# A recurrence and attention kernel: two triangular inverses, a table of side jobs and one copy rearranged

## The chip, the cores and the metric

The kernel runs on one core of a Trainium2 chip. A core has five engines that run their own instruction streams side by side and wait for each other by semaphores: TensorE (PE, matmuls and transposes), VectorE (DVE), ScalarE (ACT), GpSimd (POOL) and SyncE (SP, which issues the transfers here). The metric is the time of one execution on the device in microseconds (us). The profile comes from one execution.

## The reference

There are two parts. The first is a linear recurrence over 768 time steps, for 4 batches of 8 heads, each with a 40 x 40 state; the second is causal attention by four experts of which two are chosen per token.

```
for t in range(S):
    y[:, :, t] = np.einsum('bhd,bhde->bhe', rt, state)
    Sa = np.einsum('bhde,bhe->bhd', state, at)
    state_decay = state * wt[:, :, None, :] - np.einsum('bhd,bhe->bhde', Sa, bt)
    state = state_decay + np.einsum('bhd,bhe->bhde', vt, kt)
...
logits = x @ w_gate                       # x: y as (4, 768, 320)
topk = np.argpartition(-logits, K, axis=-1)[..., :K]
...
for e in range(E):
    q = x @ wq[e]; k = x @ wk[e]; v = x @ wv[e]
    ... causal softmax(q k^T / 8) ...
    ye = a @ v @ wo[e]
    # added to the tokens that chose e, with their weight
```

## The kernel before, in words

**Tiling.** Time is cut in 24 chunks of 32 steps; four chunks are a window, so there are 6 windows W. The 32 heads (batch x head) are 4 groups g of 8. A *unit* u = 4c + g is one chunk of one group: 96 units. Within a chunk the recurrence is written with 32 x 32 matrices: a unit needs the inverse of a triangular one for each head, and the state that the unit of the chunk before has left.

**Units.** A loop over n does one phase each of several units (MAIN): in this order u of unit n-1 (matmul with the inverse TT, L370), g of unit n (L362), y of unit n-3 (the product with the states, L390), f of unit n-2 (matmul L382, then masked on DVE, L383), the transposes t (L414), k (L351) and v of unit n-1 (L377). ACT copies between them from PSUM: GT (L364), R (L372), VU (L378), the state (L400), LS (L355, L418). The decay (L402, DVE) turns py into the output XT.

**Preps.** What a group's units of a window need is prepared beforehand, in 24 preps i = 4W + g, each a string of small pieces that have letters: `a` a scan of 528 columns (L257), `b` a copy of four of its columns, PC (L259), `c` their reciprocal (L261), `s` a second scan SC (L263), `x`/`y` two products AB (L266; `X`/`Y` the same on POOL), `p` the keys KB on POOL (L268) or `k`/`l` the same in two halves on DVE (L271), `d`/`q` copies into GL on ACT (L273), `m`/`n` eight matmuls AB by KB each (L279) with a mask on DVE into GL (L280), `o` a store of a part of GL to DRAM, Ld (L284). `w`, `v`, `e` load EW, EA and EK for the next prep: EK has one buffer.

**The inverse of a window** (`invert`): its 128 triangular matrices lie one to a partition. `L` loads Ld into MT and LT (L297, L298), then for j = 1 to 30 a row step adds a multiple of row j to the rows before it: a product (L309) and a sum (L311). The rows are split at kp = 11: the first 11 on POOL (`tp`), the others on DVE (`td`); for window 0 it is the other way round, and DVE's 11 rows are split again in two chains that are written alternately (KS = 5). `S` stores the result to DRAM (Td, L313), `R` (or `B` in window 0) loads it back, transposed, in four transfers (TT, L316).

**What sets the order.** Every engine executes its instructions in the order in which the code emits them. START is a list of the pieces ahead of the first unit (`4no` means pieces n and o of prep 4, `T28` 28 rounds of row steps). EARLY, SIDE, SIDE1 (W = 1) and SIDE2 (W = 2) are tables of pieces that are put into the loop: in SIDE tables row r stands for iteration 16(W-1) + r (row steps, `S` and `R` 16 later), and the slashes part the seven phases of an iteration; `t2` is two row steps on DVE. Phase 3 is f. POOL's row steps of window W are spread evenly over the first iterations of the window before.

**The attention part** follows from about 440 us on. A check on the inputs' spread, the *verdict* (a few small DVE instructions and a PE transpose, L871), stands at its start.

Of the kernel before, what the change touches and what calls it, by code (L numbers as in the profile page):

```python
# [137 lines left out]
def recurrence(tc, ctx, I, xT, CM, early, tail=None, KP=(11, 11, 11, 11, 11, 11)):  # L138
# [30 lines left out]
    GL = [t[:, 0:4096].rearrange("p (g n s t) -> p g n s t", g=4, n=16, s=2) for t in GF]  # L169
# [77 lines left out]
    def prep(i):  # L247

        w, g = divmod(i, NG)
        AB, sc, kb, pc = ABr[i % 4], SC[i % 12], KB[i % NKB], PC[i % 12]  # L250
        gl = GL[w % 2]
        SUF = SUFs[1 if i in (1, 3, 5) else 0]
        sv = SUF[:, 1:529].rearrange("p (n c) -> p n c", c=33)
        EW, EA, EK = (x[0:104] for x in (E8[i] if i < 8 else own))
        ea = EA.rearrange("p (n c) -> p n c", c=32)
        def f0a():
            V.tensor_tensor_scan(SUF[:, 0:528][:, ::-1], EW[:, ::-1], d1[:, ::-1], 1.0, op0=OP.mult, op1=OP.add)  # L257
        def f0b():
            V.tensor_copy(pc, sv[:, ::4, 0])  # L259
        def f0c():  # L260
            V.reciprocal(D1P[:, 0:528:132], pc)  # L261
        def f1():
            V.tensor_tensor_scan(sc.rearrange("p n c -> p (n c)"), EW, D1P, 0.0, op0=OP.mult, op1=OP.add)  # L263
        def f2(s, e=V):
            q = slice(64 * s, 64 * s + 40)
            e.tensor_tensor(AB[q, :, 32 * s:32 * s + 32], ea[q], sc[q, :, 0:32], op=OP.mult)  # L266
        def fp():
            PL.tensor_tensor(kb[0:104].rearrange("p n (k c) -> p n k c", k=2), EK.rearrange("p (n k c) -> p n k c", n=16, k=2),  # L268
                             sv[:, :, None, 1:33].to_broadcast([104, 16, 2, 32]), op=OP.mult)
        def fk(k):  # L270
            V.tensor_tensor(kb[0:104, :, 32 * k:32 * k + 32], EK.rearrange("p (n k c) -> p n k c", n=16, k=2)[:, :, k], sv[:, :, 1:33], op=OP.mult)  # L271
        def f5(s):
            A.activation(gl[64:104, g, :, s, :], AB[64 * s:64 * s + 40, :, 32 * s:32 * s + 32], AF.Copy)  # L273
        def mm(c):
            p_a = ps([64, 4, 2, 64])
            for p in range(4):
                for cc in range(2):
                    n = p * 4 + c + cc
                    T.matmul(p_a[:, p, cc, :], kb[0:104, n, :], AB[0:104, n, :], start=True, stop=True)  # L279
            V.tensor_tensor(gl[0:64, g].rearrange("q (p c) s t -> q p c s t", p=4)[:, :, c:c + 2].rearrange("q p c s t -> q p (c s) t"),  # L280
                            p_a.rearrange("q p c (s t) -> q p (c s) t", s=2), maskn[:, None, None, :].to_broadcast([64, 4, 4, 32]),
                            op=OP.mult)
        def f6():
            nc.sync.dma_start(Ld[w % 2][32 * g:32 * g + 32].rearrange("n j t -> j n t"),  # L284
                              gl[32:64, g].rearrange("q n s t -> q (n s) t"))
        def load(k):
            load_e(i + 1, k)
        return dict(a=f0a, b=f0b, c=f0c, s=f1, x=lambda: f2(0), X=lambda: f2(0, PL), y=lambda: f2(1), Y=lambda: f2(1, PL), p=fp, k=lambda: fk(0), l=lambda: fk(1),
                    d=lambda: f5(0), q=lambda: f5(1), m=lambda: mm(0), n=lambda: mm(2), o=f6,
                    w=lambda: load(0), v=lambda: load(1), e=lambda: load(2))  # L290

    def invert(w):

        L, M = LT, MT
        kp = KP[w]
        def ld():
            nc.sync.dma_start(M, Ld[w % 2])  # L297
            nc.sync.dma_start(L, Ld[w % 2][:, kp:31])  # L298
        def cp():
            PL.memset(M.rearrange("p t j -> p (t j)")[:, ::33], 1.0)  # L300
        def step(e, j, r0, r1, tmp):

            m, n = min(j, r1) - r0, 31 - j
            if m <= 0:
                return []
            tmp = tmp[:, 0:n * m].rearrange("p (t i) -> p t i", t=m)
            o = M[:, r0:r0 + m, j + 1:32]
            row = L[:, j - kp, j + 1:32] if j >= kp and r1 <= kp else M[:, j, j + 1:32]
            return [lambda: e.tensor_tensor(tmp, row[:, None, :].to_broadcast([128, m, n]),  # L309
                                            M[:, r0:r0 + m, j][:, :, None].to_broadcast([128, m, n]), op=OP.mult),  # L310
                    lambda: e.tensor_tensor(o, o, tmp, op=OP.add)]  # L311
        def st():
            nc.sync.dma_start(Td[w % 2], M)  # L313
        def bk():
            for g in range(4):
                nc.sync.dma_start(TT[w % 2][32 * g:32 * g + 32], Td[w % 2][32 * g:32 * g + 32].rearrange("n t j -> t n j"))  # L316
# [23 lines left out]
    def unit(u):  # L340
# [15 lines left out]
        def s_g():  # L356
            p_g = ps([97, 4, 40])
            for h in range(8):
                p, s = divmod(h, 2)
                o = 1024 * g + 64 * (p * 4 + cw) + 32 * s  # L360
                r = 104 * (h0 // 2 + p) + 64 * s
                T.matmul(p_g[64 * s:64 * s + 33, p], gl[:, o:o + 33], r1[:, r:r + 40], start=True, stop=True, tile_position=(0, 64 * s))  # L362
            for s in range(2):
                A.activation(gt[32 * g:32 * g + 32, s::2], p_g[64 * s:64 * s + 32], AF.Copy)  # L364
        def s_u():
            p_u = ps([97, 4, 40])
            for h in range(8):
                p, s = divmod(h, 2)
                o = 64 * (p * 4 + cw) + 32 * s
                T.matmul(p_u[64 * s:64 * s + 33, p], tt[:, o:o + 33], gt[:, h, :], start=True, stop=True, tile_position=(0, 64 * s))  # L370
            for s in range(2):
                A.activation(hd(r2[32:64, 40 * h0:40 * h0 + 320], 40)[:, s::2], p_u[64 * s:64 * s + 32], AF.Copy, scale=-1.0)  # L372
# [129 lines left out]
    for n in range(NU + 4):  # L502
# [4 lines left out]
        for s, (x, d) in enumerate(MAIN):  # L507
# [140 lines left out]
def moe(tc, ctx, I, xT, out, ident, pre, FL=None, FI=None):  # L648
# [241 lines left out]
    for n in range(N + LAG[2]):  # L890
# [78 lines left out]
```

## Time and profile before

| | us |
|---|---|
| median of 3 runs | 694.3 (690.43 to 698.01) |
| the profiled execution's own time | 693.77 |
| its span on the core | 691.9 |
| PE busy | 578.5 (84%) |
| DVE busy | 513.7 (74%) |
| ACT busy | 492.6 (71%) |
| POOL busy | 340.1 (49%) |
| last row step of window 0's inverse on DVE ends | 69.3 |
| first f on DVE (unit 0) | 90.8 |
| last row step of window 1's inverse on POOL ends | 133.5 |
| u of unit 16 (first of window 1) | 145.9 |

A row of the timeline has the start and the length of an instruction (or of a few of one kind in a row, x2), the engine, the line in the code, the operation and the tiles: output<-inputs. In brackets stands the engine's idle time before it and what ended that. SPq rows are issues of transfers, not the transfers themselves.

### The profile page before, as it was taken

The page shows a single profiled execution, that of the slowest core. Times are in us where ns is not written, and L with a number is a line of the kernel's source. Part 1 is how long each engine was busy: PE and PEld are TensorE (multiplying, and loading weights), DVE is VectorE, ACT ScalarE, POOL GpSimd, SP SyncE. Part 2 cuts the span into 40 slices and gives each one's busy share as a digit, 9 for nine tenths or more (in the row PEclk, how much of TensorE's full clock was granted, in tenths as well). Part 3 has the DMA queues.
Part 4 walks back from the last instruction along what each step waited for, and adds up shares of the span by engine and source line. Part 5 has one row for each costly group of instructions (what it writes and reads, how often), then busy time and mean ns, then how long its engine had stood idle before and what let it go on. Part 6 is the DMA issues. An engine that isn't in the chain of part 4 may idle for free. (4 is left out here: it accounts for less than half of the span.)

```text
span 691.9 us, 22434 instructions
## 1 busy us (share of the span) xinstructions
PE 578.5 (84%) x8849; PEld 504.5 (73%) x8849; DVE 513.7 (74%) x1248; ACT 492.6 (71%) x1311; POOL 340.1 (49%) x512
## 2 busy tenths in 40 slices
PE   4630687897899779879999999779989989999994
PEld 4530576786788779768988878778878877887773
DVE  8899879966976797598574576498887597667651
ACT  4593288787878688968899999457576656676662
POOL 5565469618934980785085001046456255333731
PEclk9565599999999899999999999999999999999998
DMA  7860665397467549836734993523231202202101
GB/s 195 216 164 12 139 160 131 111 191 190 121 148 213 136 114 185 212 98 149 175 94 103 247 248 85 146 51 81 76 90 34 77 24 82 71 11 56 39 30 44
DMA packets 89994, 82.09 MB, mean 119 GB/s; under 512 B 54936, under 2 KB 73112, under 8 KB 89880
## 3 DMA queue, kind: packets, MB, share of 16 engines
q1 hardware_dynamic: 89736, 80.47, 46.3%
q8 instruction: 72, 1.18, 0.7%
q14 instruction: 42, 0.34, 0.2%
q10 hardware_dynamic: 144, 0.10, 0.0%
HBM read 60.10 MB, written 14.16 MB: 107 GB/s over the span
## 5 line engine op out<-in xcount | busy, mean ns | idle before, releaser
L819 POOL TENSOR_TENSOR P<-P,m 128x128 f32<-128x128 f32 (+2 forms) x96 | 87.7, 936 | 101.5 <-DVE m L815 44.8
L390 PE MATMUL py<-R,LS 128*40 128x80 f32 x1536 | 81.3, 238 | 31.5 <-DVE R L383 14.3
L311 POOL TENSOR_TENSOR MT<-MT,TP 128x84 f32<-128x84 f32 (+13 forms) x169 | 91.7, 543 | 13.2
L390 PEld LDWEIGHTS py<-R,LS 128*40 128x40 f32 x1536 | 61.7, 119 | 39.5 <-DVE R L383 13.8
L279 PE MATMUL ps<-AB,KB 104*64 104x64 f32 x768 | 62.7, 249 | 24.0 <-DVE AB L266 9.6
L808 ACT ACTIVATE P<-sc,m 128x128 f32<-128x128 f32 (+2 forms) x96 | 60.8, 634 | 24.5 <-DVE m L807 18.1
L279 PEld LDWEIGHTS ps<-AB,KB 104*64 104x64 f32 x768 | 57.7, 161 | 27.6 <-issue 9.4
L807 DVE TENSOR_REDUCE m<-sc 128x1 f32<-128x128 f32 (+2 forms) x96 | 59.3, 621 | 20.7 <-PE sc L800 19.5
L364 ACT ACTIVATE GT<-ps 32x160 f32<-32x160 f32 x192 | 56.6, 295 | 19.5 <-PE ps L362 15.3
L382 PE MATMUL ps<-RB,VU 128*64 128x64 f32 x768 | 63.2, 227 | 4.2 <-ACT VU L378 3.3
L797 PE MATMUL sc<-ks,qs 128*128 128x384 f32 (+4 forms) x256 | 62.1, 344 | 4.8 <-ACT P L808 4.6
L383 DVE TENSOR_TENSOR R<-ps,CM 64x256 f32<-64x256 f32 x96 | 39.5, 411 | 28.6 <-PE ps L382 27.5
L372 ACT ACTIVATE R<-ps 32x160 f32<-32x160 f32 x192 | 56.7, 295 | 5.2 <-PE ps L370 2.0
L382 PEld LDWEIGHTS ps<-RB,VU 128*64 128x64 f32 x768 | 53.8, 140 | 8.5 <-ACT VU L378 7.3
L309 POOL TENSOR_TENSOR TP<-LT,MT 128x220 f32<-128x220 f32 (+9 forms) x100 | 53.2, 532 | 7.8
L400 ACT ACTIVATE R<-py 40x160 f32<-40x160 f32 x144 | 42.9, 298 | 16.2 <-PE py L390 13.1
L827 PE MATMUL pt<-CM,P 128*128 128x128 f32 x336 | 51.8, 275 | 1.8 <-ACT pt L833 1.7
L355 ACT ACTIVATE LS<-pt 64x320 f32<-64x320 f32 x96 | 41.6, 433 | 14.8 <-PE pt L351 13.4
L370 PE MATMUL ps<-GT,TT 128*33 128x40 f32 x1536 | 49.9, 208 | 1.4 <-DMA TT<-Td 0.9
L418 ACT ACTIVATE LS<-pt 40x320 f32<-40x320 f32 x92 | 39.6, 431 | 11.9 <-PE pt L414 10.1
L797 PEld LDWEIGHTS sc<-ks,qs 128*128 128x128 f32 x256 | 40.4, 189 | 9.7 <-ACT P L808 8.3
L362 PE MATMUL ps<-R,GLe 128*33 128x40 f32 x768 | 26.1, 207 | 23.2 <-issue 21.7
(150 smaller groups left out, 1440.0 us busy)
## 6 DMA issues: line engine op xcount, KB each, us to landing
RB<-in_RB SPq DMA_DIRECT2D x24, 320.0 KB
EK<-in_EK SPq DMA_DIRECT2D x18, 416.0 KB
ks<-ks SPq DMA_DIRECT2D x32, 192.0 KB
R<-in_VG SPq DMA_DIRECT2D x24, 208.0 KB
EW<-in_EA SPq DMA_DIRECT2D x18, 214.5 KB
R<-in_VT SPq DMA_DIRECT2D x48, 80.0 KB
R<-in_RT SPq DMA_DIRECT2D x24, 160.0 KB
xT<-XT SPq DMA_DIRECT2D x48, 80.0 KB
```

What stands on the lines that cost most here:

```text
L279: T.matmul(p_a[:, p, cc, :], kb[0:104, n, :], AB[0:104, n, :], start=True, stop=True)
L309: return [lambda: e.tensor_tensor(tmp, row[:, None, :].to_broadcast([128, m, n]), M[:, r0:r0 + m, j][:, :, None].to_broadcast([128, m, n]) ...
L311: lambda: e.tensor_tensor(o, o, tmp, op=OP.add)]
L364: A.activation(gt[32 * g:32 * g + 32, s::2], p_g[64 * s:64 * s + 32], AF.Copy)
L372: A.activation(hd(r2[32:64, 40 * h0:40 * h0 + 320], 40)[:, s::2], p_u[64 * s:64 * s + 32], AF.Copy, scale=-1.0)
L382: T.matmul(p_f[:, 2 * p:2 * p + 2], vu[:, p, :], rb[:, 4 * g + p, :], start=True, stop=True)
L390: T.matmul(py[64 * s:64 * s + 40, p], ls[:, h, :], m, start=True, stop=True, tile_position=(0, 64 * s))
L797: T.matmul(ps[:, c, 0:cw], QS[b][:, e, o], KS[b][:, e, z, k], start=(z == 0), stop=(z == 1 and not last), skip_group_check=True)
L807: V.tensor_reduce(m[:, 0, t:t + 1], ps[:, 0:ch, 0:cw], axis=AX.XY, op=OP.max, negate=True)
L808: later(DE, lambda: A.activation(pv, ps[:, 0:ch, 0:cw], AF.Exp, bias=m[:, 0, t:t + 1], accum_out=m[:, 1, t:t + 1]))
L819: PL.tensor_tensor(P[:, 0:n], P[:, 0:n], m[:, 3, t:t + 1].to_broadcast([128, n]), op=OP.mult)
L827: T.transpose(p[:, 128 * y:128 * y + 128], st["P"][t][:, 128 * c:128 * c + 128], ident)
```

## The change

1. **Window 0's inverse** on DVE is one chain of rows 0 to 10 in place of two alternating ones, and the rounds hold two steps each of DVE and POOL. In START, pieces 6a and 6b stood ahead of it and 6p on POOL beside it; they are now behind it. Lines from 257 on shift by up to three.
2. **GL is ordered by chunk** (column block 8 x chunk + 4s + p, in place of 2 x (4p + chunk) + s). The masks of `m`/`n` write one contiguous block. The reload of TT for window 0 is cut by chunk: four transfers for the first chunk's eight matrices, then four for the rest. The matmuls of u read 33 columns from their offset, as before.
3. **Pieces of preps 6 and 7** (window 1) in EARLY come one iteration later, behind the first units; SIDE1's `L` goes from row 2 to 3 and `C` from 6 to 7.
4. **SIDE and SIDE2**: the KB halves `k`, `l` of prep 1 of the window go from row -11 to row -10, and its `y` the other way; `1e` and `3e` move within an iteration or by one.
5. **The PC copy** (`b`) is done by ACT from prep 8 on, and the reciprocal reads the scan's columns itself.
6. **Side jobs of a phase f** are emitted ahead of the decay of the same iteration, not behind.
7. **The verdict** is emitted at step 30 of the attention's loop, not ahead of it.

```diff
-T28 S B 4m 6cspx 4dno 6Y 7a E8 7b 5d 7c 5q 7spYx k0 5nm"""
+T30 S B 4m 6abcspx 4dno 6Y 7a E8 7b 5d 7c 5q 7spYx k0 5nm"""
 EARLY = {
-    0: "/7d//7q/6nm 5o/6q/7m",
-    1: "6o 7n////7o",
+    1: "/7d///6nm 5o//6q",
+    2: "7q///6o/7m//7n 7o",
...
-    -11: "///1k t1 1l t1///1w",
-    -10: "///1y t3/t2//1ve",
+    -11: "///1y t3/t2//1w",
+    -10: "///1k t1 1l t1///1ve",
...
         def f0b():
-            V.tensor_copy(pc, sv[:, ::4, 0])
+            if i < 8:
+                V.tensor_copy(pc, sv[:, ::4, 0])
+            else:
+                A.activation(pc, sv[:, ::4, 0], AF.Copy)
         def f0c():
-            V.reciprocal(D1P[:, 0:528:132], pc)
+            V.reciprocal(D1P[:, 0:528:132], sv[:, ::4, 0])
...
         def bk():
-            for g in range(4):
-                nc.sync.dma_start(TT[w % 2][32 * g:32 * g + 32], Td[w % 2][32 * g:32 * g + 32].rearrange("n t j -> t n j"))
+            for z in ((slice(0, 32),) if w else (slice(0, 8), slice(8, 32))):
+                for g in range(4):
+                    q = slice(32 * g, 32 * g + 32)
+                    nc.sync.dma_start(TT[w % 2][q, z], Td[w % 2][q][z].rearrange("n t j -> t n j"))
...
-                x, y = (step(V, j, r, q, (TP[1], flat(KB[8]))[k]) for k, (r, q) in enumerate(((0, KS), (KS, kp))))
-                td += x[:1] + y[:1] + x[1:] + y[1:]
-                tp += step(PL, j, kp, 32, TP[0])
+                td += step(V, j, 0, kp, TP[0])
+                tp += step(PL, j, kp, 32, TP[1])
...
-                    for x in td, td, td, td, tp, tp:
+                    for x in td, td, tp, tp:
...
+            for f in jobs.get((n, s), []):
+                f()
             if x == "f" and decay:
                 decay()
                 decay = None
-            for f in jobs.get((n, s), []):
-                f()
...
-    if FL is not None:
+    def verdict():
...
+        if FL is not None and n == 30:
+            verdict()
```

On SP, behind the reload of window 0's inverse (TT), stand the stores of window 1's preps (Ld), loads for preps 8 and 9 (EW, EK, EA) and the load of window 1's matrices (MT). Before:

```order
L316 DMA TT_119<-Td_139 32x32x32 [waits DMAHW5_49]
L284 DMA Ld_138<-GL_114 32x32x32 [waits DMAHW6_49,DVE_49]
L201 DMA EW_82<-in_EA 104x528 [waits DMAHW7_49]
L201 DMA EK_84<-in_EK 104x1024 [waits DMAHW0_49,Pool_49]
L201 DMA EA_83<-in_EA 104x512 [waits Pool_49]
L284 DMA Ld_138<-GL_114 32x32x32 [waits DMAHW2_49,DVE_49]
L284 DMA Ld_138<-GL_114 32x32x32 [waits DMAHW3_49,DVE_49]
L284 DMA Ld_138<-GL_114 32x32x32 [waits DMAHW4_49,DVE_49]
L201 DMA EW_82<-in_EA 104x528 [waits DMAHW7_49,DMAHW5_49,DVE_49]
L297 DMA MT_116<-Ld_138 128x1024 [waits DMAHW4_49,DMAHW6_49,DMAHW3_49,DMAHW2_49]
```

The same place after the change:

```order
L320 DMA TT_119<-Td_139 32x24x32
L286 DMA Ld_138<-GL_114 32x32x32 [waits DMAHW2_49,DVE_49]
L200 DMA EW_82<-in_EA 104x528 [waits DMAHW3_49]
L200 DMA EK_84<-in_EK 104x1024 [waits DMAHW4_49,Pool_49]
L200 DMA EA_83<-in_EA 104x512 [waits DMAHW5_49,Pool_49]
L286 DMA Ld_138<-GL_114 32x32x32 [waits DMAHW6_49,DVE_49]
L200 DMA EW_82<-in_EA 104x528 [waits DMAHW7_49,DMAHW3_49,DVE_49]
L286 DMA Ld_138<-GL_114 32x32x32 [waits DMAHW0_49,DVE_49]
L200 DMA EK_84<-in_EK 104x1024 [waits DMAHW4_49,DMAHW1_49,DVE_49]
L200 DMA EA_83<-in_EA 104x512 [waits DMAHW2_49,DMAHW5_49,DVE_49,Pool_49]
L286 DMA Ld_138<-GL_114 32x32x32 [waits DVE_49]
L299 DMA MT_116<-Ld_138 128x1024 [waits DMAHW6_49,DMAHW3_49,DMAHW0_49]
```

EK and EA of prep 9 have moved ahead of the last store and the load of MT.

On DVE, at iterations 21 and 22, from the f of unit 19 (R_125) past that of unit 20 (the first R_126) stand the KB halves of prep 13 (KB_102), its second product (AB_110), row steps of window 2 (TP, MT) and decays (XT). Before:

```order
L383 TENSOR_TENSOR R_125<-ps,CM 64x256
L402 TENSOR_TENSOR XT_132<-py_78,SC_96 104x4x32
L311 TENSOR_TENSOR MT_116<-MT_116,TP_118 128x2x18
L271 TENSOR_TENSOR KB_102<-EK_84,SUF_86 104x16x32 x2
L309 TENSOR_TENSOR TP_118<-MT_116 128x51
L383 TENSOR_TENSOR R_126<-ps,CM 64x256
L402 TENSOR_TENSOR XT_132<-py_79,SC_96 104x4x32
L311 TENSOR_TENSOR MT_116<-MT_116,TP_118 128x3x17
L309 TENSOR_TENSOR TP_118<-MT_116 128x64
L266 TENSOR_TENSOR AB_110<-EA_83,SC_93 40x16x32
```

After:

```order
L386 TENSOR_TENSOR R_125<-ps,CM 64x256
L313 TENSOR_TENSOR MT_116<-MT_116,TP_118 128x2x18
L268 TENSOR_TENSOR AB_110<-EA_83,SC_93 40x16x32
L405 TENSOR_TENSOR XT_132<-py_78,SC_96 104x4x32
L311 TENSOR_TENSOR TP_118<-MT_116 128x51
L313 TENSOR_TENSOR MT_116<-MT_116,TP_118 128x3x17
L386 TENSOR_TENSOR R_126<-ps,CM 64x256
L311 TENSOR_TENSOR TP_118<-MT_116 128x64
L273 TENSOR_TENSOR KB_102<-EK_84,SUF_86 104x16x32 x2
L405 TENSOR_TENSOR XT_132<-py_79,SC_96 104x4x32
```

The halves have gone behind the f of unit 20, the product ahead of it, and each decay behind the pieces of its iteration.

On ACT, at iteration 19, is the run of one unit's copies and the place where the next one's begin. Before:

```order
L378 ACTIVATE VU_128<-ps 80x256
L372 ACTIVATE R_125<-ps 32x4x40 x2
L364 ACTIVATE GT_136<-ps 32x4x40 x2
L400 ACTIVATE R_124<-py_78 40x4x40 x2
L355 ACTIVATE LS_121<-pt 64x320
L355 ACTIVATE LS_122<-pt 64x320
L378 ACTIVATE VU_127<-ps 80x256
```

After:

```order
L381 ACTIVATE VU_128<-ps 80x256
L375 ACTIVATE R_125<-ps 32x4x40 x2
L367 ACTIVATE GT_136<-ps 32x4x40 x2
L403 ACTIVATE R_124<-py_78 40x4x40 x2
L261 ACTIVATE PC_92<-SUF_86 104x4
L358 ACTIVATE LS_121<-pt 64x320
L358 ACTIVATE LS_122<-pt 64x320
L381 ACTIVATE VU_127<-ps 80x256
```

The copy of PC stands between the state copies and the next unit's LS and VU.

More of the change, by code (lines that the diff above doesn't have):

```diff
@@ L21 @@
 START = """Z0 E4 0apbc E5 0sx 1a 1b 0y 1c 0d 1sx 2a 0n E7 0q E6 1py 0m 2b 0o 1d 2pcs 1n R1 1q 2x 3a 2Yq 1m 3b 2m 3p
-2d 3csx 1o 3y 2n 4a 3m 2o 4pb 3n 4c 5a 3d 4sy 3o 5b L 3q R0 4x R2 V00 V10 5cs V11 5xp 6a C 5y V01 Z1 4q T2 6b
-T28 S B 4m 6cspx 4dno 6Y 7a E8 7b 5d 7c 5q 7spYx k0 5nm"""
+2d 3csx 1o 3y 2n 4a 3m 2o 4pb 3n 4c 5a 3d 4sy 3o 5b L 3q R0 4x R2 V00 V10 5cs V11 5xp C 5y V01 Z1 4q
+T30 S B 4m 6abcspx 4dno 6Y 7a E8 7b 5d 7c 5q 7spYx k0 5nm"""
 EARLY = {
-    0: "/7d//7q/6nm 5o/6q/7m",
-    1: "6o 7n////7o",
+    1: "/7d///6nm 5o//6q",
+    2: "7q///6o/7m//7n 7o",
     3: "///6d",
@@ L46 @@
     -2: "/R//3y/1m//1nodq 3v",
-    -1: "////2m//2nodq",
-    0: "/3e///3m//3nodq",
+    -1: "/3e///2m//2nodq",
+    0: "////3m//3nodq",
     1: "L",
@@ L63 @@
     -1: "/R",
-    2: "L",
-    6: "C",
+    3: "L",
+    7: "C",
 }
@@ L71 @@
     -12: "///t1 1s t1//1x",
-    -11: "/t1//t1 1kl/t1//1w",
-    -10: "1e///t2/t3/1y",
+    -11: "/t1//t1/t2//1w",
+    -10: "///t1 1kl/t2/1y/1e",
     -9: "//2a/t1 2bc t1 2s/1v//t1",
@@ L86 @@
 }
-KS = 5
 POOLT = {0: (4, 12), 1: (4, 10), 2: (4, 12)}
@@ L168, in recurrence @@
     GF = [ep.tile([128, 4104], F32, name="GLe")] + ring("GL", [128, 4104], 1)
-    GL = [t[:, 0:4096].rearrange("p (g n s t) -> p g n s t", g=4, n=16, s=2) for t in GF]
+    GL = [t[:, 0:4096].rearrange("p (g n t) -> p g n t", g=4, n=32) for t in GF]
     LT = ring("LT", [128, 20, 32], 1)[0]
@@ L188, in recurrence @@
     hd = lambda t, d: t.rearrange("p (h d) -> p h d", d=d)
-    g1 = GL[1][:, 2:4].rearrange("p g n s t -> p (g n s t)")
+    g1 = GL[1][:, 2:4].rearrange("p g n t -> p (g n t)")
     own = (EWr[0], EAr[0], EKr[0])
@@ L230, in zgl @@
     def zgl(i):
-        zero(GL[i][96:128].rearrange("p g n s t -> p (g n s t)"))
+        zero(GL[i][96:128].rearrange("p g n t -> p (g n t)"))
     def rest(x):
@@ L272, in f5 @@
         def f5(s):
-            A.activation(gl[64:104, g, :, s, :], AB[64 * s:64 * s + 40, :, 32 * s:32 * s + 32], AF.Copy)
+            A.activation(gl[64:104, g].rearrange("q (c s p) t -> q c s p t", c=4, s=2)[:, :, s],
+                         AB[64 * s:64 * s + 40, :, 32 * s:32 * s + 32].rearrange("q (p c) t -> q c p t", c=4), AF.Copy)
         def mm(c):
-            p_a = ps([64, 4, 2, 64])
-            for p in range(4):
-                for cc in range(2):
+            p_a = ps([64, 2, 2, 4, 32])
+            for cc in range(2):
+                for p in range(4):
                     n = p * 4 + c + cc
[L279 to L282, printed above, removed]
+                    T.matmul(p_a[:, cc, :, p], kb[0:104, n, :], AB[0:104, n, :], start=True, stop=True)
+            V.tensor_tensor(gl[0:64, g, 8 * c:8 * c + 16], p_a.rearrange("q c s p t -> q (c s p) t"),
+                            maskn[:, None, :].to_broadcast([64, 16, 32]), op=OP.mult)
         def f6():
             nc.sync.dma_start(Ld[w % 2][32 * g:32 * g + 32].rearrange("n j t -> j n t"),
-                              gl[32:64, g].rearrange("q n s t -> q (n s) t"))
+                              gl[32:64, g])
         def load(k):
@@ L359, in s_g @@
                 p, s = divmod(h, 2)
-                o = 1024 * g + 64 * (p * 4 + cw) + 32 * s
+                o = 1024 * g + 32 * (8 * cw + 4 * s + p)
                 r = 104 * (h0 // 2 + p) + 64 * s
@@ L368, in s_u @@
                 p, s = divmod(h, 2)
-                o = 64 * (p * 4 + cw) + 32 * s
+                o = 32 * (8 * cw + 4 * s + p)
                 T.matmul(p_u[64 * s:64 * s + 33, p], tt[:, o:o + 33], gt[:, h, :], start=True, stop=True, tile_position=(0, 64 * s))
```

## Prediction

> **What bounds the kernel now.** I read the page first: busy times, then the slices (17.3 us each).
>
> ```profile
> span 691.9 us, 22434 instructions
> PE 578.5 (84%) x8849; PEld 504.5 (73%) x8849; DVE 513.7 (74%) x1248; ACT 492.6 (71%) x1311; POOL 340.1 (49%) x512
> PE   4630687897899779879999999779989989999994
> DVE  8899879966976797598574576498887597667651
> PEclk9565599999999899999999999999999999999998
> ```
>
> PE leads from the eighth slice on, and from about 440 us (the attention part) it is busy almost throughout; so what the recurrence ahead of it gains or loses reaches the end. In slices 0 to 4 PE is half idle and DVE full: there the start's chain on DVE decides. The timeline of DVE shows it, from the first group's inverse (L309, L311) to the first f (L383).
>
> ```profile
> 44.16 1.24 DVE L257 TENSOR_TENSOR_SCAN SUF<-EW,D 104x528 f32<-104x528 f32 x1
> 48.74 0.15 DVE L259 COPY PC<-SUF 104x4 f32<-104x4 f32 x1
> 61.20 2.22 DVE L309 TENSOR_TENSOR KB<-LT,MT 128x78 f32<-128x78 f32 x1
> 63.48 0.23 DVE L311 TENSOR_TENSOR MT<-MT,KB 128x78 f32<-128x78 f32 x1
> 69.17 0.17 DVE L311 TENSOR_TENSOR MT<-MT,KB 128x6 f32<-128x6 f32 x1
> 82.08 0.68 DVE L280 TENSOR_TENSOR GL<-ps,CM 64x512 f32<-64x512 f32 x1 [0.71 <-PE ps L279]
> 84.36 0.68 DVE L280 TENSOR_TENSOR GL<-ps,CM 64x512 f32<-64x512 f32 x1 [1.60 <-PE ps L279]
> 90.84 0.42 DVE L383 TENSOR_TENSOR R<-ps,CM 64x256 f32<-64x256 f32 x1
> ```
>
> The inverse ends at 69.25; DVE reaches f 21.6 us later, idle for only 2.31 (0.71 + 1.60). What follows the start is the inverse of window 1, seen on POOL, SP and PE: load, a POOL chain of 40 us, store, reload, unit 16.
>
> ```profile
> 61.16 2.17 POOL L268 TENSOR_TENSOR KB<-EK,SUF 104x1024 f32<-104x1024 f32 x1
> 69.40 0.34 SPq L313 DMA_DIRECT2D Td<-MT  x1
> 72.00 2.44 SPq L316 DMA_DIRECT2D TT<-Td  x4
> 88.84 0.34 SPq L297 DMA_DIRECT2D MT<-Ld  x1
> 93.48 0.24 POOL L309 TENSOR_TENSOR TP<-MT 128x30 f32<-128x30 f32 x1 [3.94 <-DMA MT<-Ld]
> 133.50 0.35 SPq L313 DMA_DIRECT2D Td<-MT  x1
> 137.57 5.26 SPq L316 DMA_DIRECT2D TT<-Td  x4
> 145.94 0.48 PE L370 MATMUL ps<-GT,TT 128*33 128x40 f32 x16 [0.91 <-DMA TT<-Td]
> ```
>
> At 145.94 unit 16 waits for TT while PE already stands: a second deadline that the first units don't set. Third, the list of waits sent me to DVE's L271 (KB halves waiting for EK), which comes once in each later window:
>
> ```profile
> 157.15 0.96 SPq L201 DMA_DIRECT2D EK<-in_EK  x1
> 161.01 0.41 DVE L383 TENSOR_TENSOR R<-ps,CM 64x256 f32<-64x256 f32 x1
> 165.47 1.68 DVE L271 TENSOR_TENSOR KB<-EK,SUF 104x512 f32<-104x512 f32 x2 [3.75 <-DMA EK<-in_EK]
> 229.42 0.69 DVE L271 TENSOR_TENSOR KB<-EK,SUF 104x512 f32<-104x512 f32 x1 [3.88 <-DMA EK<-in_EK]
> 292.56 0.77 DVE L271 TENSOR_TENSOR KB<-EK,SUF 104x512 f32<-104x512 f32 x1 [3.26 <-DMA EK<-in_EK]
> 168.06 0.88 PE L390 MATMUL py<-R,LS 128*40 128x80 f32 x16 [3.45 <-issue]
> core 0: us, PE busy (x) PEld busy (x) DVE busy (x) ACT busy (x) POOL busy (x), PEclk, DMA share, GB/s
> 168.00:172.30 4.30, 4.12 (x64) 3.75 (x64) 4.13 (x9) 2.17 (x7) 3.83 (x7) 0.60 0.33 100
> 231.50:235.00 3.50, 3.48 (x36) 3.22 (x38) 3.33 (x7) 1.03 (x3) 3.11 (x6) 0.50 0.19 53
> 90.00:95.00 5.00, 3.47 (x84) 3.14 (x85) 3.23 (x8) 2.88 (x8) 1.21 (x5) 1.00 0.85 252
> ```
>
> While DVE stands at L271, the next f is queued behind it, PE's y behind that f: PE is empty for 3.45 us and then gets a clock of 0.60 and 0.50. DVE is full in the 4.3 us behind (4.13), so it can't make the loss good.
>
> **The change part by part.** The profiled execution took 693.77 us (span 691.9, 1.9 around it), near the median of 694.3 (690.43 to 698.01); the sum is made against 693.8.
>
> Start. Scan 6a (1.24) and copy 6b (0.15) go behind the inverse, and so does POOL's 6p, beside which one step took 2.22 and not about 0.23: -1.24 - 0.15 - 2.0. One chain has about half the instructions but each waits for the one before. The rows give 0.15 to 0.23 per small instruction, in pairs of two chains; I take +0.5 for the loss of overlap (-0.5 to +1.5). The inverse ends 2.9 earlier, at about 66.3. Behind it 6a and 6b come back (+1.4), and 6p may block DVE there once more (+2); two masks (L280, 1.36), the copy 8b (0.17) and the idle 2.31 leave the stretch ahead of the first f. -2.9 + 1.4 + 2.0 - 1.36 - 0.17 - 2.31 = -3.3: first f at about 87.5. [...]
>
> The split load in eight pieces brings no more: TT's issue ends by 74.4 (72.00 + 2.44), unit 0's last matmul reads one column past its chunk and so needs all eight, and DVE is what holds the first f. Cost of four more issues at 0.61 each (2.44 / 4): 2.4 us of SP, ahead of loads that wait anyway; 0 (0 to +1).
>
> Unit 16. The masks 7m, 7n and store 7o of window 1 now stand behind the first units. Before, the MT load went out 2.0 ahead of the first f (88.84 against 90.84); now f ends at 87.9, the masks behind it (0.68 each, one partly beside f's wait) at about 88.8, and the store has to land, 2.6 as from Td to TT at the start (69.40 to 72.00): 91.4, 2.6 later. SP also issues EK and EA ahead of it now. From issue to POOL's first step took 4.64 (93.48 - 88.84); with the port and DMA less crowded I take 3.6 (3.3 to 4.6): 95.0. Plus 40.0 to the store (93.48 to 133.50): 135.0 to 135.3, against 133.50. The reload's issue was then held up on SP (4.07 between Td and TT); here I take the start's 2.6: 137.9, unit 16 at 146.4, +0.5 (-1 to +2). So the 3.3 us of the start end as idle PE ahead of unit 16, 0.9 + 3.3 + 0.5 = 4.7 us. Row 168.06 shows what such a gap costs: 4.3 x (1 - 0.60) = 1.7 of PE time behind it. The row at 90 shows the other side: full clock behind a gap of 2 us. I take +1.7 (0 to 2): the term is +2.2.
>
> [...]
>
> Windows 2 to 4: the KB halves k, l go one row later, y one row earlier. Without the stall, f of unit 20 comes about 3.2 behind 161.01 (what bounds the units there is ACT, below), and k, l behind it:
>
> ```profile
> 152.06 0.38 ACT L378 ACTIVATE VU<-ps 80x256 f32<-80x256 f32 x1
> 153.72 0.62 ACT L400 ACTIVATE R<-py 40x160 f32<-40x160 f32 x2
> 155.27 0.38 ACT L378 ACTIVATE VU<-ps 80x256 f32<-80x256 f32 x1
> 152.00:155.30 3.30, 3.29 (x83) 2.88 (x78) 1.34 (x3) 3.08 (x11) 2.03 (x2) 1.00 0.55 178
> 153.21 0.42 DVE L383 TENSOR_TENSOR R<-ps,CM 64x256 f32<-64x256 f32 x1 [2.15 <-PE ps L382]
> 154.59 1.25 DVE L257 TENSOR_TENSOR_SCAN SUF<-EW,D 104x528 f32<-104x528 f32 x1
> L259 DVE COPY PC<-SUF 104x4 f32<-104x4 f32 x9 | 1.7, 191 | 0.2
> ```
>
> 161.01 + 3.2 + 0.4 for f + 0.5 of steps = 165.1, and EK is there at about 165.4: just met. Removed: 3.75, 3.88 and 3.26.
>
> Against it stand ACT's new copies. In the order ACT now has L261 between L403 and the next unit's L358 and L381, waiting for the scan. f at 153.21 ends at 153.6, the scan directly behind it at about 154.8; ACT is free at 154.34: 0.46 of waiting in an engine that goes through a unit in 3.2 us (152.06 to 155.27) and is busy for 3.08 of the 3.30 around it, with VU, hence f, queued behind. Three such copies in a window lie in its unit chain: 1.4. Beside POOL and the steps the moved halves cost 1.68 for two, against 0.69 alone: 0.3, and y next to them 0.1. DVE saves one copy of 0.19 in its full stretch. Per window: 3.75 + 0.19 - 1.4 - 0.4 = 2.1, likewise 2.3 and 1.7: -6.1 (-1.5 if each copy costs about 1 us, -10.9 if none does). The decays now behind the scans (step order) cost nothing while their PSUM is free: L402 idles today for ACT anyway; 0 (-1 to +1).
>
> The verdict ahead of the attention part: its PE transpose moves into n == 30.
>
> ```profile
> 441.44 0.27 PE L871 MATMUL pt<-CM,fl 128*1 128x128 f32 x1 [1.01 <-DVE fl L869]
> 444.76 0.74 ACT L678 ACTIVATE ws<-wo 128x640 fp32r<-128x640 f32 x1 [6.32 <-DMA wo<-in_WO]
> ```
>
> The 1.01 goes, but the wait for wo ends at 444.76 either way: -0.5 (0 to -1).
>
> Sum: +2.2 - 6.1 - 0.5 = -4.4; 693.8 - 4.4 = 689.4, put at 689.
>
> **The rivals.** A: the stall goes through whole. ACT's waits hide because DVE, full at 4.13 of 4.30, is what bounds behind n = 20, and unit 16 comes no later: 693.8 - 10.9 = 683; with the clock also held up, 680. For it: PE at 0.60 and 0.50 recovers its clock too, and PE is just as full as ACT around 153 (3.29 of 3.30), so a short wait of ACT may find cover. Against it: ACT is as good as full there (3.08 of 3.30).
>
> B, slower: the scan is not directly behind f but behind the steps and f of a full DVE, so that every copy on ACT holds the next VU by about 1.6 (0.34 of a step and 1.25 of scan), and the loop f, y, ACT, VU, f turns at that pace. Twelve copies in windows 2 to 4 make 19.2; less 10.9 and 0.5, plus 2.2: +10.0, 704. It decides from 0.77 a copy (9.2 / 12). For it: the single engine order puts L261 ahead of VU. Against it: the change also emits the scan ahead of the decay, straight behind f.
>
> C: window 1's load goes out as early as before, since the POOL chain finds MT unhindered; then the start's 3.3 flow through and no clock is lost: 693.8 - 3.3 - 6.1 - 0.5 = 684.
>
> D: the change doesn't do what it says: k and l meet EK unlanded one row later too (165.1 against 165.4 is close, and more DMAs are ahead of it), or the stall reappears at the next consumer. Then the windows give about -1 in all, beside +2.2 and -0.5: 694.5.
>
> **How the numbers follow.** Forecast 0.38 (686 to 693), A 0.28, C 0.10, D 0.12, B 0.12. A difference under 1% (687.4 to 701.2 against 694.3) can hardly be told from none here. Faster by over 1%: A, C and about a seventh of the forecast, 0.43. Slower: most of B, 0.10. The rest 0.47. The range goes from A with the clock (680) up past D to 697, leaving out most of B and a little at the low end.
>
> **What would show it.** The inverse's last DVE step near 66 and the first f near 87.5; the MT load of window 1 issued near 91 and unit 16's matmul waiting 4 to 5 us for TT with a clock under 1 behind it; no wait for EK at DVE's KB halves and no 3.4 us gap on PE at units 20, 36 and 52; ACT's L261 waiting about 0.5 each. Wrong would be: L261 waiting over 0.8, the load of MT going out before 89, or the gap on PE coming back a unit later.

## The result, and the profile after

The changed kernel takes 704.0 us (median of 4 runs, 703.2 to 704.8) against 696.2 for the kernel before in the same comparison: a ratio of 1.0107, with a 95% interval of 1.0064 to 1.015. It is slower by about 1%, where 689 had been forecast. The profiled execution took 703.24 us against 693.77, so 9.5 us have to be found. A run over 1.5% above the fastest of its kernel is left out of the ratios here; below this concerns one run of 711.3 us, of the copies with the new order.

The page after, with the same rows as were shown of before:

```profile
span 701.5 us, 22365 instructions
PE 589.1 (84%) x8849; PEld 513.8 (73%) x8849; DVE 512.2 (73%) x1182; ACT 495.7 (71%) x1327; POOL 335.9 (48%) x512
PE   4630585998899879987999999979989989999995
DVE  8999966887866986796584576478887587668651
PEclk9565697999799999999999999989999999999998
```

DVE has less to do than before (512.2 against 513.7) and yet the span has grown by 9.6: it waits more. PE's busy time is up by 10.6 with the same 8849 matmuls, and the clock row has new sevens (0.7); the mean granted clock is 0.921 against 0.940: part of its work was done at a lower clock.

Where the time came from is best seen unit by unit. This table was worked out from the two traces: it has the start of each unit's f on DVE (L383 before, L386 after).

| f of unit | before | after | difference |
|---|---|---|---|
| 0 | 90.84 | 86.25 | -4.59 |
| 6 | 110.56 | 108.49 | -2.07 |
| 7 | 113.76 | 117.23 | +3.47 |
| 16 | 150.45 | 153.83 | +3.38 |
| 21 | 171.87 | 169.10 | -2.77 |
| 25 | 186.46 | 185.85 | -0.61 |
| 28 | 197.01 | 200.86 | +3.85 |
| 37 | 235.22 | 234.74 | -0.48 |
| 44 | 260.81 | 266.09 | +5.28 |
| 53 | 298.43 | 299.39 | +0.96 |
| 60 | 323.97 | 331.04 | +7.07 |
| last | 439.20 | 446.03 | +6.83 |

The two gains that the change was made for come, and both are lost again. The first unit comes 4.6 us early, and at unit 7 5.5 us go. In each later window 4.3 to 6.2 us are won by units 21, 37 and 53, where the stall was, and 5.8 to 6.6 lost by units 28, 44 and 60. The attention part adds 2.8 (9.6 of span less 6.8).

**Unit 7.** The timelines of DVE and POOL after the change, and one row of a table of windows (busy time of PE, its loads, DVE, ACT and POOL in a stretch, then the granted clock and the transfers):

```profile
110.41 0.70 DVE L311 TENSOR_TENSOR TP<-MT 128x91 f32<-128x91 f32 x1
116.24 0.48 DVE L313 TENSOR_TENSOR MT<-MT,TP 128x91 f32<-128x91 f32 x1 [5.13 <-POOL MT L302]
117.23 0.41 DVE L386 TENSOR_TENSOR R<-ps,CM 64x256 f32<-64x256 f32 x1
115.44 0.56 POOL L313 TENSOR_TENSOR MT<-MT,TP 128x176 f32<-128x176 f32 x1
116.06 0.15 POOL L302 MEMSET MT<- 128x32 f32 x1
116.13 0.48 POOL L311 TENSOR_TENSOR TP<-LT,MT 128x165 f32<-128x165 f32 x1
118.00:122.00 4.00, 4.00 (x44) 3.72 (x42) 3.90 (x10) 1.14 (x4) 3.69 (x5) 0.50 0.52 113
```

L302 is piece C, the ones on MT's diagonal. In SIDE1 it went from row 6 to row 7, and in POOL's queue that puts ten row-step instructions ahead of it. POOL does it at 116.06 (at 107.52 before). DVE's row step L313 writes the same tile, is emitted behind the memset, and waits 5.13 us for an instruction of 0.15; the f of unit 7 is queued behind it. PE gets nothing for 6.02 us (to 117.69) and is then at a clock of 0.50 for 4 us (the window's row).

**Units 26 to 28.** ACT's new copies and what follows from the last of a window, on ACT, DVE and PE:

```profile
ACT PC L261 <- DVE SUF L256: 22.6, 15, 3.8
142.50 0.21 ACT L261 ACTIVATE PC<-SUF 104x4 f32<-104x4 f32 x1 [0.60 <-DVE SUF L256]
157.18 0.21 ACT L261 ACTIVATE PC<-SUF 104x4 f32<-104x4 f32 x1 [0.49 <-DVE SUF L256]
171.46 0.21 ACT L261 ACTIVATE PC<-SUF 104x4 f32<-104x4 f32 x1 [1.23 <-DVE SUF L256]
187.61 0.21 ACT L261 ACTIVATE PC<-SUF 104x4 f32<-104x4 f32 x1 [2.63 <-DVE SUF L256]
185.85 0.41 DVE L386 TENSOR_TENSOR R<-ps,CM 64x256 f32<-64x256 f32 x1
186.33 1.24 DVE L256 TENSOR_TENSOR_SCAN SUF<-EW,D 104x528 f32<-104x528 f32 x1
190.31 0.42 DVE L386 TENSOR_TENSOR R<-ps,CM 64x256 f32<-64x256 f32 x1 [2.35 <-PE ps L385]
189.16 1.12 PE L385 MATMUL ps<-RB,VU 128*64 128x64 f32 x8 [2.10 <-ACT VU L381]
189.00:194.00 5.00, 4.84 (x64) 4.56 (x66) 3.63 (x8) 3.90 (x13) 4.45 (x8) 0.50 0.26 66
```

The first row is from the list of waits: 22.6 us in 15 waits, the longest 3.8. ACT is through with its state copies at 184.98 and stands 2.63 us until the scan of a DVE that runs behind has ended. Behind the copy are LS (0.88) and VU (0.38); PE's L385 needs VU and stood 2.10; DVE, the full engine here (busy for 5.60 of the 5.8 us from 180), needs PE and stands 2.35. The next 5 us PE runs at 0.50.

**The stall itself** is gone. After the change the KB halves follow the f of unit 20 without a wait:

```profile
165.88 0.42 DVE L386 TENSOR_TENSOR R<-ps,CM 64x256 f32<-64x256 f32 x1 [0.82 <-PE ps L385]
166.23 0.21 DVE L311 TENSOR_TENSOR TP<-MT 128x64 f32<-128x64 f32 x1
166.36 1.28 DVE L273 TENSOR_TENSOR KB<-EK,SUF 104x512 f32<-104x512 f32 x2
```

### The profile page after: what moved, and what is told of

It is laid out like the page before. It is cut to its first block, busy times and chain, and to the rows that moved or that the text cites. A ratio compares the mean times of both kernels' runs of the same rounds, so it can differ in the third digit from the quotient of the medians.

```text
span 701.5 us, 22365 instructions
## 1 busy us (share of the span) xinstructions
PE 589.1 (84%) x8849; PEld 513.8 (73%) x8849; DVE 512.2 (73%) x1182; ACT 495.7 (71%) x1327; POOL 335.9 (48%) x512
## 3 DMA queue, kind: packets, MB, share of 16 engines
q8 instruction: 72, 1.18, 0.7%
## 5 line engine op out<-in xcount | busy, mean ns | idle before, releaser
L393 PE MATMUL py<-R,LS 128*40 128x80 f32 x1536 | 84.6, 244 | 14.7 <-DVE R L386 8.6
L313 POOL TENSOR_TENSOR MT<-MT,TP 128x84 f32<-128x84 f32 (+13 forms) x169 | 90.4, 535 | 13.3
L385 PE MATMUL ps<-RB,VU 128*64 128x64 f32 x768 | 64.5, 229 | 22.9 <-ACT VU L381 20.3
L386 DVE TENSOR_TENSOR R<-ps,CM 64x256 f32<-64x256 f32 x96 | 39.7, 414 | 60.0 <-PE ps L385 59.0
L393 PEld LDWEIGHTS py<-R,LS 128*40 128x40 f32 x1536 | 64.4, 123 | 21.5 <-DVE R L386 9.3
L385 PEld LDWEIGHTS ps<-RB,VU 128*64 128x64 f32 x768 | 54.7, 142 | 29.3 <-ACT VU L381 26.4
L810 DVE TENSOR_REDUCE m<-sc 128x1 f32<-128x128 f32 (+2 forms) x96 | 59.4, 622 | 20.6 <-PE sc L803 19.2
L311 POOL TENSOR_TENSOR TP<-LT,MT 128x220 f32<-128x220 f32 (+9 forms) x100 | 51.5, 515 | 7.8
L313 DVE TENSOR_TENSOR MT<-MT,TP 128x19 f32<-128x19 f32 (+22 forms) x125 | 45.0, 360 | 8.3 <-POOL MT L302 5.1
L373 PEld LDWEIGHTS ps<-GT,TT 128*33 128x33 f32 x1536 | 38.2, 117 | 16.2 <-issue 5.7
```

What stands on the lines that cost most here:

```text
L385: T.matmul(p_f[:, 2 * p:2 * p + 2], vu[:, p, :], rb[:, 4 * g + p, :], start=True, stop=True)
L393: T.matmul(py[64 * s:64 * s + 40, p], ls[:, h, :], m, start=True, stop=True, tile_position=(0, 64 * s))
L810: V.tensor_reduce(m[:, 0, t:t + 1], ps[:, 0:ch, 0:cw], axis=AX.XY, op=OP.max, negate=True)
```

## The experiments

All were timed in three rounds against the kernel before on the same chip; the ratios are to that kernel, with 95% intervals, and the differences in us are of the medians where nothing else is said. Each text says whether an edit is made on the kernel before or on the changed one.

**Are the copies on ACT the loss at units 26 to 28?** On the changed kernel, one line back:

```diff
-            if i < 8:
-                V.tensor_copy(pc, sv[:, ::4, 0])
-            else:
-                A.activation(pc, sv[:, ::4, 0], AF.Copy)
+            V.tensor_copy(pc, sv[:, ::4, 0])
```

> The changed kernel with the PC copies of all preps on DVE again (the reciprocal still reads the scan). Theory A: ACT's copy waits for a scan that stands behind row steps on a full DVE (2.6 us at unit 26), holds VU, and two units later PE's clock is halved; that is 4 to 6 us in each of windows 2, 3 and 4, less 0.2 each for the copy on DVE: 690 to 694. Rival S: the loss at units 26 to 28 is DVE's own full stretch giving the stall's gain back, then it stays at 702 to 705.

Measured: 697.8 us, ratio 1.0017 (0.9988 to 1.0046); the changed kernel had 1.0107. The copies take 0.9%, some 6 us, of it. From unit 16 to the end of the recurrence this profile wins 6.8 us against before, where the changed kernel loses 3.45: a difference of 10.3 in one pair of profiles, against 6.3 by the medians. Between 189 and 194 us, where the changed kernel had a clock of 0.50, PE is full at full clock:

```profile
189.00:194.00 5.00, 5.00 (x108) 4.68 (x103) 4.62 (x10) 4.13 (x13) 4.61 (x6) 1.00 0.65 174
```

The rival that DVE's full stretch gives the gain back has fallen as an account of the whole loss; part of it stands, since without the copies, too, +0.16 at unit 21 becomes +3.17 at unit 28 and +4.14 at unit 32. The time came out 4 above what theory A gave at most: it had put the copies at 4 to 6 us in each of three windows, and by the medians they take some 6 in all.

**Each of the two table and engine edits alone, on the kernel before.** The halves (SIDE shown; SIDE2 likewise, with 1e and 3e):

```diff
-    -11: "///1k t1 1l t1///1w",
-    -10: "///1y t3/t2//1ve",
+    -11: "///1y t3/t2//1w",
+    -10: "///1k t1 1l t1///1ve",
```

> The kernel before with nothing changed but the tables: the KB halves one row later, y one row earlier, 1e and 3e as in the change. Theory: the wait for EK goes (3.75, 3.88, 3.26 in windows 2 to 4) and without ACT's copies the gain stays, 6 to 7 us by the recurrence's end, about 689 against 695.7. Rival S: DVE's full stretch behind the stall gives it back by unit 32, then within 1 us of before.

Measured: 691.7 us, 0.9928 (0.9899 to 0.9958), that is -5.3 us. That is less than the 6 to 7 that were expected, and rival S has a part in it: in the profile -2.56 at unit 21 is +0.39 at unit 31, and the next two windows go the same way (-3.11 to -0.62, -3.12 to -1.39). The wait list has 1.8 us left of 12.3:

```profile
DVE KB L271 <- DMA EK<-in_EK: 1.8, 4, 0.8
```

The rows from the f of unit 21 to that of unit 31, before and with the halves alone, show where the gain goes:

```profile
171.90:211.50 39.60, 34.89 (x764) 32.12 (x761) 34.01 (x82) 32.13 (x90) 22.17 (x36) 1.00 0.61 147
169.30:211.90 42.60, 37.14 (x780) 34.08 (x775) 37.35 (x83) 33.58 (x93) 26.11 (x43) 0.96 0.55 135
```

DVE doesn't wait longer there; it is busy for 3.3 us more with 83 instructions and not 82, while POOL does 3.9 us more. Its three products AB (L266) take 1.18 us each and not 0.81. POOL's row steps, which went on while DVE stood for EK (POOL was busy for 9.60 of the 10.9 us from 161 before), now run beside a full DVE; whether the products are longer for that, no run takes apart.

The copies on ACT and the reciprocal from the scan, alone:

> The kernel before with only the PC copies of preps 8 and on moved to ACT (and the reciprocal reading the scan). Theory A: each window has one copy that ACT waits 2 us or more for, with a halved clock behind it, 3.4 us a window as between the changed kernel and the one with the copies on DVE: 10 us, about 705 against 695.7. Rival: it hurts only where the KB halves come late (together with the table's change), because the stall gives ACT time: 695 to 697.

Measured: 710.5 us, 1.0193 (1.0141 to 1.0245), that is +13.5 us, the largest effect of all, and with the stall still in place; the rival that the two only hurt together has fallen. The wait list and the row of the line, sixteen copies of 0.21 us with 33.5 us of waiting ahead of them:

```profile
ACT PC L262 <- DVE SUF L257: 33.5, 15, 4.9
L262 ACT ACTIVATE PC<-SUF 104x4 f32<-104x4 f32 x16 | 3.3, 208 | 33.5 <-DVE SUF L257 33.5
```

**Is it the extra instruction on ACT or its place?** The halves as above, and the copies on ACT, but each emitted in a later iteration's phase (the letter b moves; one row of several shown):

```diff
-    -13: "///1abc",
-    -12: "///1s t1 1x t1",
+    -13: "///1ac",
+    -12: "///1bs t1 1x t1",
```

> The kernel before with the tables of the KB halves and with the PC copies on ACT, but each emitted in the phase f of the next or a later iteration, when its scan is long done. Theory A says the copy costs ACT its own 0.2 us and no wait: as the halves alone or 1 us below, 688 to 689. If what hurts is ACT's extra instruction and not its place, it is 3 us or more above the halves alone.

Measured: 690.8 us, 0.9892 (0.9855 to 0.9929), -6.2 us. The same sixteen instructions now wait 1.2 us in all:

```profile
L262 ACT ACTIVATE PC<-SUF 104x4 f32<-104x4 f32 x16 | 3.3, 209 | 1.2 <-DVE SUF L257 0.8
```

So the place was the cost. Taking the copies off DVE is worth no more than can be told: 0.9892 against 0.9928 for the halves alone, with overlapping intervals.

**The step order.** On the kernel before, alone and then with the copies:

```diff
+            for f in jobs.get((n, s), []):
+                f()
             if x == "f" and decay:
                 decay()
                 decay = None
-            for f in jobs.get((n, s), []):
-                f()
```

> The kernel before with only the step order changed: side jobs of phase f ahead of the decay. Theory: L402 idles for ACT's state copies for 19.7 us in all, now other work goes first; where DVE isn't the bound this is worth nothing: within 2 us of before. Rival: it is a gain of 3 us or more of its own, or the later decay holds py and costs as much.

Measured: 698.3 us, 1.0035 (0.9999 to 1.0072): +2.4 us by the ratio (the medians differ by 3.4), not clear of none, and surely no gain.

> The kernel before with the PC copies on ACT and the new step order together. Copies alone cost 13.5 us with waits of 33.5 us at L262; in the changed kernel they cost 6.3 with 22.6. Theory: the new order puts the scan straight behind f and takes the decay's wait for ACT out of the way of the scan that ACT waits for: 6 to 8 us over before. Rival: the difference is due to the KB halves' stall being gone, then 12 or more over before.

Measured: 701.9 us (median of three runs, 700.3 to 706.1), 1.0106 (1.0036 to 1.0176), that is +7.4 us by the ratio. The waits fall from 33.5 to 27.9 us. It points to the order taking away some of what the copies cost (+13.5 alone, and 0 to +5 for the order alone), which would fit the 6 us that they cost in the changed kernel; the intervals of 1.0106 and 1.0193 overlap, so this isn't settled.

```profile
ACT PC L262 <- DVE SUF L257: 27.9, 15, 4.2
```

**The memset at unit 7.** On the changed kernel:

```diff
     3: "L",
-    7: "C",
+    6: "C",
```

> The changed kernel with one number put back: in SIDE1 the diagonal memset of window 1's MT (C) at row 6 again, not 7. Theory M: the memset stands ten POOL instructions later in the changed kernel and DVE's next row step, written behind it, waits 5.1 us for it; put back, that wait and the 5.5 us by which the f of unit 7 falls behind are gone: about 698.5 against 704.0. Rival: the wait is due to POOL's chain starting late (its load of MT is issued at 91.6 and not 88.8), then the same DVE step waits for POOL anyway and the time stays at 703 to 704.

Measured: 705.4 us, 1.0119 (1.0083 to 1.0156): no gain. The forecast of theory M failed, and so did the rival's reason. The wait at unit 7 does go, and f of unit 14 is at +0.22 against before and not at +3.13; but unit 16 is at +3.30 all the same:

```profile
138.75 6.36 SPq L320 DMA_DIRECT2D TT<-Td  x4
147.90 0.75 PE L373 MATMUL ps<-GT,TT 128*33 128x40 f32 x16 [2.65 <-DMA TT<-Td]
```

PE now stands 2.65 us for window 1's inverse, which had been hidden behind the memset's loss. With both edits at once:

> Both edits at once: memset at row 6 and PC copies on DVE. If the two losses are separate they add: about 704.0 - 5.5 - 12 = 686.5, that is below the kernel before. If the earlier arrival of unit 7 is absorbed by the wait for window 1's inverse at unit 16, only 690 to 692.

Measured: 698.6 us, 1.0038 (1.0019 to 1.0058), no better than the copies alone (1.0017). Neither forecast was met. The two don't add: two causes hold unit 16 at the same place, and taking one away shows the other (PE stands 2.76 us for window 1's inverse in this profile, too).

**What of the start makes window 1 late?** The start alone, everything else as in the kernel before:

> The start alone: inverse as one chain, 6a, 6b, 6p behind it, chunk layout, split reload, EARLY one iteration later, L and C of window 1 one later; KB halves, PC copies, step order and verdict as in the kernel before. Theory U: the load of window 1's matrices goes out at 91.6 to 94.6 and not 88.8, so unit 16 comes 3 to 5 us later, and nothing gives that back: 699 to 700 against 695.7. Rival: the first units' gain of 4 us reaches the end: 692.

Measured: 702.3 us, 1.0069 (1.0039 to 1.0099), +5.3 us. Then the same, with the tables EARLY and SIDE1 as before:

```diff
-    1: "/7d///6nm 5o//6q",
-    2: "7q///6o/7m//7n 7o",
+    0: "/7d//7q/6nm 5o/6q/7m",
+    1: "6o 7n////7o",
...
-    3: "L",
-    7: "C",
+    2: "L",
+    6: "C",
```

> The start alone as in the run before, but with EARLY and SIDE1's L and C as in the kernel before: the chain, 6a, 6b, 6p behind it, the chunk layout and the split reload stay. Theory U: what costs in the start is that window 1's masks, store and load come behind the first units; put back, the load of MT goes out at 89 or earlier, unit 16 comes no later than before, and the time is 695 to 697 (against 702.3). Rival: the loss is the chain, the layout or the eight transfers themselves, then 700 or more.

Measured: 695.4 us, 1.0004 (0.9975 to 1.0032). The two issues of window 1's load, of the start alone and then with the old tables:

```profile
94.33 0.35 SPq L296 DMA_DIRECT2D MT<-Ld  x1
88.03 0.34 SPq L296 DMA_DIRECT2D MT<-Ld  x1
```

So the chain, the moved scan and copy, the layout and the eight transfers together are worth nothing that can be measured, and the loss is the later places of window 1's pieces (EARLY, L and C together; C alone brought nothing above, and EARLY and L were not taken apart). Of the 6.3 us between the two issues some 3 seem to be chance: the changed kernel, with the same start, issued this load at 91.57 (the last section shows how far profiles of one start differ). With the old places the first f is at 90.40, as before (90.84): the 4.6 us by which the changed kernel's first f was early came from those places too, and were gone again by unit 16.

**The verdict.** Ahead of the loop again, in the changed kernel:

> The changed kernel with the verdict ahead of the attention's loop again. Theory V: moving it shifted the start of the attention (a cast of xh that DVE did early comes late, PE waits twice and gets a clock of 0.83): 2 to 3 us, so 701 to 702. Rival: the 2.3 us between the end of the recurrence and the first output matmul are chance of that execution: 704.

Measured: 703.9 us, 1.0096 (1.0059 to 1.0134): nothing. Theory V has fallen. The attention part of this profile is 2.0 us longer than before's with the same code, and it came out between 1.7 shorter and 3.6 longer in the profiles of the other runs. What sets that was not found.

**All but the two places.** The changed kernel with the copies emitted later, EARLY and SIDE1's L and C as before, and the verdict ahead of the loop:

> The changed kernel with its PC copies emitted a phase or more later, EARLY and SIDE1's L and C as before, and the verdict ahead of the loop: chain, layout, split reload, halves, step order and copies on ACT stay. If the two losses were these, it is the gain of the halves and later copies (6.2) and no loss at the start: about 690 against 697, or below if the start's gain reaches unit 16. If it is above 694, something else of the start costs.

Measured: 687.9 us, 0.9898 (0.9861 to 0.9935), -6.9 us against 694.9, with the run of the later copies (0.9892) the fastest. The waits that are left:

```profile
DVE KB L273 <- DMA EK<-in_EK: 3.7, 4, 1.8
ACT PC L261 <- DVE SUF L256: 1.4, 3, 0.6
```

## Why the prediction was wrong

Three terms of the sum failed, each by some 3 to 4 us: the worth of the stall, the copies and the start.

**The stall: the right wait, at twice its worth.** The wait for EK was there, 3.75 + 3.88 + 3.26 = 10.9 us in the profile, and the change removes it. The sum counted it in full, since a DVE that is full behind the stall "can't make the loss good"; less the 0.4 a window that the moved halves cost, this is 9.7. The halves alone bring 5.3 us by the medians. The step that failed is that premise: the pace of the full stretch is not fixed, and without the stall it takes 42.6 us where it took 39.6 (the rows shown with that run). That the total for these windows was put at about half of the stall is no merit of the forecast, which took the other half off for the copies. Rival A's 683, which had the stall go through whole, was out of reach.

**The copies: the wait taken from the wrong stretch.** The prediction took one place, the f at 153.21 of an ACT-bound unit, worked out a wait of 0.46 for it, and put three of those in each window: 1.4. That place was right: the waits are 0.49, 0.48 and 0.48 there in the three windows. The other nine copies from 142 to 319 us wait 0.60 to 3.79; all twelve wait 19.2 us, 1.6 each, and with the four earlier ones it is 22.6. The error was to take ACT's position against DVE from a stretch where DVE waits for ACT. Where DVE is full it runs behind, ACT is ready ahead of the f, and waits for what is left of DVE's steps, the f and the whole scan. Net of the copy that DVE saves the term was 3.6; by the medians the copies take some 6 in the changed kernel, and with the new order 7.4 in the kernel before.

Rival B had just this mechanism at 1.6 a copy, 19.2, and 704 us; it was given 0.12. The mechanism and the waits were right, but that its sum met the time is luck: of 22.6 us of waiting some 6 reached the end, it took the stall's 10.9 as all gained and left the start at +2.2, and these errors largely cancel.

**Unseen in the forecast: the circle.** The copy puts DVE's scan between DVE's f and the next f: f, scan, copy, LS, VU, matmul, f. From 185.85 to 190.31 that is 4.46 us, against 2.25 for the same two f's before (186.46 to 188.71). A full engine thus waits for itself, and PE's clock falls as well (0.50 from 189 to 194 us). Rival B alone named such a loop.

**The start: the load right, the loss at another place and larger.** The load of MT was forecast at 91.4 and went out at 91.57; POOL's first step at 95.0 and 95.32; the first f at 87.5 and 86.25. The step came 3.75 after the issue (4.64 before); the forecast's 3.6 was put down to a less crowded port and DMA. No run shows a crowded port; the DMA share in these two stretches was 0.72 against 0.86. The 2.0 of 6p came back behind the inverse, as put: beside it (POOL, 67.23 to 69.40) DVE's scan L265 at 67.47 took 3.04 us, and at 81.25, with POOL idle, 1.26.

```profile
91.57 0.35 SPq L299 DMA_DIRECT2D MT<-Ld  x1
95.32 0.66 POOL L311 TENSOR_TENSOR TP<-MT 128x30 f32<-128x30 f32 x1 [10.97 <-DMA MT<-Ld]
133.26 0.34 SPq L315 DMA_DIRECT2D Td<-MT  x1
139.70 3.83 SPq L320 DMA_DIRECT2D TT<-Td  x4
148.10 0.48 PE L373 MATMUL ps<-GT,TT 128*33 128x40 f32 x16
144.00:148.00 4.00, 4.00 (x89) 3.73 (x87) 3.21 (x8) 3.84 (x10) 0.00 (x0) 1.00 0.98 189
```

From there the path was another one. POOL's chain took 37.9 us and not 40.0, and the store went out at 133.26, forecast at 135.0 to 135.3 and at 133.50 in the kernel before. The reload's issue was put at 137.9 and came at 139.70, behind other issues on SP. But PE is full at full clock in the 4 us ahead of unit 16, which comes at 148.10 without a wait: of the 4 to 5 us of waiting for TT that were forecast, with a clock under 1 behind, the changed kernel shows nothing. It had lost the time at unit 7 already, where DVE waited for the memset. What the prediction didn't price at all is this move of C by one row: it named SP's queue and not POOL's. The wait that was forecast stands behind it and shows, with 2.65 us, once C is back at row 6; so taking the memset's wait away alone brought nothing. The term was +2.2 and the runs of the start alone give +5.3 (+3.4 at unit 16 in the changed kernel's profile, +3.3 with the memset back).

**The terms put at nothing.** The chain and the split reload: right, by the start with the old tables (1.0004). The step order was put at 0 (-1 to +1) and measured 0 to +5. **The verdict**, -0.5, measured 0. That the 1.01 us ahead of the attention part was covered by the wait for wo may be so; the runs can't tell.

**The sum.** By the runs apart: start +5.3, halves -5.3, copies with the new order +7.4, is +7.4; the whole change is +7.9. The prediction had +2.2 for the start, -9.7 for the halves, +3.6 for the copies and -0.5 for the verdict, -4.4. So the miss of 12.3 is some 3 at the start, 4.4 at the stall and 3 to 4 at the copies; no one of them alone would have led out of the range. Another 2.4 of the way from 689 to 704 are the kernel before, which had 696.2 in this comparison and not the 693.8 that the sum started from.

## What to carry to other kernels

An instruction moved to another engine takes a place in that engine's queue: what counts isn't its 0.2 us but the wait for its input (33.5 us for the sixteen copies alone), with all that stands behind it, and this wait has to be taken from the stretch where the engine that makes the input is behind, not from where it is ahead. Emitted one iteration later the same instructions wait for next to nothing (1.2 us in all). A wait that is removed need not be worth its length: 10.9 us of it brought 5.3. And where a gain at one place has vanished, look for a second deadline there: removing one of two waits that end at the same time shows nothing until the other is gone too.

## What was not expected of the hardware

PE's clock didn't come back at the same point after the same work. In the changed kernel and in the one with the copies on DVE the instructions are the same up to prep 8's copy at about 81 us, and PE does the same in the windows from 75 to 83 us: nearly idle (0.44 and 0.79 us of the first 4), then full (4.00 of the next 4). The kernel with the verdict moved back has the changed kernel's instructions throughout the recurrence. The rows are of 79 to 83 and 83 to 87 us, first of the changed kernel, then of the one with the copies on DVE, with two later rows of it; the last row is of the one with the verdict moved back:

```profile
79.00:83.00 4.00, 4.00 (x37) 3.88 (x38) 3.93 (x5) 0.21 (x1) 1.15 (x2) 0.54 0.24 37
83.00:87.00 4.00, 2.91 (x64) 2.53 (x62) 3.62 (x7) 3.67 (x9) 1.35 (x1) 1.00 0.57 103
79.00:83.00 4.00, 4.00 (x35) 3.88 (x36) 3.93 (x6) 0.00 (x0) 1.08 (x2) 0.50 0.25 37
83.00:87.00 4.00, 3.23 (x47) 2.75 (x46) 3.21 (x5) 3.34 (x8) 1.37 (x1) 0.50 0.54 105
87.00:91.00 4.00, 4.00 (x37) 3.72 (x36) 1.10 (x2) 0.71 (x3) 0.00 (x0) 0.50 0.48 144
91.00:95.00 4.00, 4.00 (x65) 3.88 (x64) 2.37 (x6) 2.40 (x7) 0.00 (x0) 0.51 0.24 37
83.00:87.00 4.00, 3.74 (x54) 3.42 (x53) 3.62 (x6) 3.35 (x8) 1.36 (x1) 0.50 0.53 110
```

After 4 us of full work the first has a clock of 1.00 and the other two stay at 0.50, and their unit 1 comes 4.3 and 3.0 us later. The one with the copies on DVE then does another 8 us of full work (87 to 95) at 0.50 and 0.51. What decides when the clock comes back, no run here shows. For a reader of profiles it means that the first 100 us of a single profile of this kernel are worth 4 us either way, which is more than several of the effects above: the medians of many runs had to decide.
